# Attention and a gated MLP on one core: a list schedule with tuned ranks, and a literal order of all 2531 operations

## The chip, the core and the metric

One core of a Trainium2 chip runs the whole kernel as one program. Its engines run side by side, each in the order of its own instructions: TensorE (PE in the profile) multiplies matrices into PSUM, VectorE (DVE) and ScalarE (ACT) work element by element, GpSimd (POOL) does some elementwise work from SBUF, and SyncE (SP) issues the DMAs. They wait for one another by semaphores. The metric is the device time of one execution in microseconds.

## The reference

Inputs: q, k, v of (4, 8, 576, 64): four batches, eight heads, 576 positions, 64 channels; weights w_gate and w_val (512 x 1536) and w_out (1536 x 512), all fp32.

- q and k are rotated by position (RoPE: halves x1, x2 become x1 cos - x2 sin, x1 sin + x2 cos);
- scores = q k^T / 8, softmax over keys, times v, for each of the 32 heads;
- the heads are joined to x of 2304 x 512;
- out = (sigmoid(x w_gate) * (x w_val)) w_out, 2304 x 512.

## The kernel before, in words

**Numbers.** Nearly all matrix products run in fp16 with a high and a low half of each operand (three products a term), and each half is made by two elementwise steps: a "high" step that scales and rounds (line 476 on ACT or line 478 on DVE) and a "rest" step that subtracts (line 482, always DVE). Batch 0 is special: its scores and its first GLU half run on fp32 operands, while the weights are still being decoded.

**Stages.** For each batch b and head pair p, `keys_queries` loads q and k with a swapped copy, multiplies by cos (line 703, for batch 0 line 695) and by sin (705; batch 0 makes the swapped copy by a matrix product, line 690, and line 692), adds (707; 697), finds a scale (714, 717), splits into halves and moves them into `stk` by DMA. `attention` takes row tiles t of 128 queries: scores (765), a row minimum on DVE (788), exp on ACT (793), the sum's reciprocal on DVE (797, 799), high and rest of the probabilities (`softmax`, the call at 803), a transposing DMA into `pt` (944), then 30 products with v into the one PSUM bank `pv` (953) and its eviction on ACT and DVE. `hidden(b, f, i)` makes one of 12 blocks of the GLU for half i of a batch's tokens: 12 products for the gate into a bank of `m` (three banks), tanh on ACT (1018), 12 products for the value into another bank, (1 + tanh) * value on DVE (1021), high (the call at 1027) and rest. `project` makes one 128-token tile of the output, 36 products (1046), eviction, DMA out. For batch 0 the first half of the queries goes through `front` and `back` (lines 822 to 928): row maxima (826), a bias product (842, 876), transposed scores (881), exp (887), products with v and with ones (902), a reciprocal (912) and x in fp32 (914, 928). Meanwhile `w_in_chunk` loads 12 chunks of 1 MB of the two input weights, which arrive as 64-bit words, decodes them in two ACT-or-DVE passes (488; 496 on ACT or 493 on DVE) and a DVE join (500), and squares them on PE (519) for a scale (`w_in_scales`); `w_out_decode` does the same for w_out.

**What sets the order.** Nothing is issued as the functions run. Every operation is registered in a `Plan` with its engine, a rank, the tokens that it reads and writes, and a function that issues it; there are 2531. `Plan.order` is a list schedule: it steps through time with costs written in the kernel (`c_dve`, `c_act` and so on), and each engine that is free takes the ready operation of lowest rank. The ranks are those of the calls, moved by a table `SHIFT` of 285 numbers, one for each call of a stage function; `LEAD` moves loads; `SIDE` has a bit for each operation that may run on either of two engines (`alt`: ACT or DVE for a high step, GpSimd or DVE for the rotations). `emit` then issues the operations in the order of their planned starts. The buffers of five pools (`m`, `s`, `p32`, `th`, `p16`) are handed out as the plan goes. On the chip the planned times have no force: each engine has its list, and semaphores for the data.

Of the kernel before, what the change touches and what calls it, by code (L numbers as in the profile page):

```python
# [61 lines left out]
class Plan:  # L62


    HOP = 0.036
    TAIL = {"DVE": 0.085, "ACT": 0.1, "POOL": 0.05, "PE": 0.165, "SP": 0.0}
    OWN = {"DVE": 0.12, "POOL": 0.13}
    ENTER, LEAVE, SWAP = 0.096, 0.2, 0.25
    FIRST, WINDOW = 1.9, 3.41333

    def __init__(self):
        self.tasks, self.preds, self.wrote, self.read = [], [], {}, {}
        self.leases = []
        self.shift, self.side, self.alts, self.lead = 0.0, 0, 0, 0.0

    def add(self, where, rank, reads, writes, fn, land=0.0, port=False, also=(), mode=None):


        n = len(self.tasks)
        rank += self.shift  # L80
        held = {x for x in (*reads, *writes, *also) if isinstance(x, Lease)}
        for x in held:
            x.users.append(n)
        self.leases.append(held)
        pre = set()
        for r in reads:
            if r in self.wrote:
                pre.add(self.wrote[r])
        for w in (*writes, *also):
            if w in self.wrote:  # L90
                pre.add(self.wrote[w])
            pre.update(self.read.get(w, ()))
        for r in reads:
            self.read.setdefault(r, []).append(n)
        for w in writes:
            self.wrote[w], self.read[w] = n, []
        pre.discard(n)
        self.tasks.append((where, rank, fn, land, port, mode))
        self.preds.append(sorted(pre))

    def order(self):
        N = len(self.tasks)
        succ = [[] for _ in range(N)]
        left = [len(p) for p in self.preds]
        for n, p in enumerate(self.preds):
            for m in p:
                succ[m].append(n)
        free, wait, ready, done = {}, {}, {}, [None] * N
        slots, parked = {}, {}
        for held in self.leases:  # L110
            for x in held:
                slots.setdefault(x.pool, {n: 0.0 for n in range(len(x.bufs))})
                x.left = len(x.users)

        def obtain(n, t):

            need = {}
            for x in self.leases[n]:
                if x.n is None:
                    need.setdefault(x.pool, []).append(x)  # L120
            late = t
            for pool, xs in need.items():
                best = sorted((f, k) for k, f in slots[pool].items())[:len(xs)]
                if len(best) < len(xs):
                    parked.setdefault(pool, []).append(n)
                    return None
                late = max(late, best[-1][0])
            if late > t:
                return late
            for pool, xs in sorted(need.items()):  # L130
                for x, (f, k) in zip(sorted(xs, key=lambda x: x.users[0]), sorted((f, k) for k, f in slots[pool].items())):
                    x.n = k
                    del slots[pool][k]
            return t

        def release(n):
            for x in self.leases[n]:
                x.left -= 1
                if not x.left:
                    slots[x.pool][x.n] = max(done[m][1] + done[m][2] + self.TAIL[done[m][0]] for m in x.users) + self.HOP  # L140
                    for m in parked.pop(x.pool, []):
                        offer(m)

        def offer(n):
            for e, _ in self.tasks[n][0]:
                t = 0.0
                for m in self.preds[n]:
                    e0, end, land = done[m]
                    if land:
                        end += land + self.HOP  # L150
                    elif e0 == e:
                        end += self.OWN.get(e, 0.0)
                    else:
                        end += self.TAIL[e0] + self.HOP
                    t = max(t, end)
                heapq.heappush(wait.setdefault(e, []), (t, self.tasks[n][1], n))
                ready.setdefault(e, [])
                free.setdefault(e, 0.0)

        for n in range(N):  # L160
            if not left[n]:
                offer(n)
        starts, bus, drain, port, last = [], self.FIRST, 0.0, 0.0, None
        slow, busy = {0: True}, {}

        def run(t, cost):

            w = int(t / self.WINDOW)
            while cost > 1e-9:
                if w not in slow:  # L170
                    k = max(slow)
                    while k < w:
                        x = busy.get(k, 0.0) / self.WINDOW
                        slow[k + 1] = x < (0.46 if slow[k] else 0.25)
                        k += 1
                u = min(cost, max(0.0, (w + 1) * self.WINDOW - t) * (0.5 if slow[w] else 1.0))
                busy[w] = busy.get(w, 0.0) + u
                cost -= u
                t += u * (2.0 if slow[w] else 1.0)
                w += 1  # L180
            return t
        while len(starts) < N:
            best = None
            for e in free:
                w, r = wait[e], ready[e]
                while w and done[w[0][2]]:
                    heapq.heappop(w)
                while r and done[r[0][1]]:
                    heapq.heappop(r)
                if r or w:  # L190
                    t = free[e] if r else max(free[e], w[0][0])
                    if best is None or t < best[0]:
                        best = (t, e)
            t, e = best
            w, r = wait[e], ready[e]
            while w and w[0][0] <= t:
                _, rank, n = heapq.heappop(w)
                if not done[n]:
                    heapq.heappush(r, (rank, n))

            held = e in ("DVE", "POOL") and port > t + 0.2
            fit = [x for x in r if not held or (e == "DVE" and not self.tasks[x[1]][4])]
            if fit:
                x = min(fit)
                r.remove(x)
                heapq.heapify(r)
            else:
                x = heapq.heappop(r)
            n = x[1]
            got = obtain(n, t)  # L210
            if got != t:
                if got is not None:
                    heapq.heappush(w, (got, x[0], n))
                continue
            where, rank, fn, land, locks, mode = self.tasks[n]
            cost = dict(where)[e]
            if e == "PE":
                if mode != last:
                    t += self.ENTER if last is None else self.LEAVE if mode is None else self.SWAP
                last = mode  # L220
            if e == "POOL" or (e == "DVE" and locks):
                t = max(t, port)
                port = t + cost
            end = run(t, cost) if e == "PE" else t + cost
            if land:

                if mode:
                    bus = max(bus, t + 1.1, drain - 0.3) + land[0]
                    end = max(end, drain + 0.1)
                else:  # L230
                    bus = max(bus, t + 1.0) + land[0] * (0.67 if t < 40 else 1.0)
                    drain = max(drain, bus + land[1])
                done[n] = (e, end, bus + land[1] - end)
            else:
                done[n] = (e, end, 0.0)
            free[e] = end
            starts.append((t, n, e))
            release(n)
            for m in succ[n]:
                left[m] -= 1  # L240
                if not left[m]:
                    offer(m)
        self.done = done
        return sorted(starts)

    def emit(self):
        self.starts = self.order()
        for t, n, e in self.starts:
            self.tasks[n][2](e)


# [79 lines left out]
def rope_attention_then_sigmoid_glu(ctx: ExitStack, tc: tile.TileContext, qk, v, w_in, w_out, tables, out):  # L331
# [59 lines left out]
    P = Plan()  # L391
# [14 lines left out]
    def op(e, us, rank, reads, writes, fn, port=False):  # L406
        P.add(((e, us),), rank, reads, writes, lambda _: fn(eng.get(e)), port=port)
# [14 lines left out]
    def dma(rank, reads, writes, kb, fn, also=(), load=False, more=0.0):  # L422
        if load:
            rank += P.lead
# [239 lines left out]
    slots = {}  # L664
# [560 lines left out]
```

## Time and profile before

| | us |
|---|---|
| median of 3 runs (664.24 to 665.35) | 665.19 |
| the profiled execution | 665.45 |
| its span, first to last instruction | 663.7 |
| PE busy in the span | 638.0 |
| DVE busy | 515.1 |
| ACT busy | 345.5 |
| POOL busy | 79.8 |

An engine's busy time is the union of its instructions. The rows further down name an engine, a line of the kernel, what is written from what is read, and a count; a bracket behind a row gives the engine's idle time ahead of it and who ended it.

### The profile page before, as it was taken

What the parts mean: (1) busy time and instruction counts of PE and PEld (TensorE: products, weight loads), DVE (VectorE), ACT (ScalarE), POOL (GpSimd) and SP (SyncE); (2) the same over time, 40 slices, a digit from 0 to 9 for tenths busy, and PEclk for the clock granted to TensorE, in tenths of its full rate; (3) what the DMA queues carried; (4) which work ended last, traced back from release to release, by engine and by line L of the source; (5) the groups of instructions that cost most, each with busy time, mean ns of one, the idle gap of its engine ahead of it and who ended that gap; (6) DMA issues with size and microseconds to landing.
All of it is one profiled execution on the core that took longest, in us unless ns stands there. A gap on an engine that the chain in (4) does not pass through costs nothing.

```text
span 663.7 us, 12849 instructions
## 1 busy us (share of the span) xinstructions
PE 638.0 (96%) x4914; PEld 439.8 (66%) x4914; DVE 515.1 (78%) x1211; ACT 345.5 (52%) x711; POOL 79.8 (12%) x85
## 2 busy tenths in 40 slices
PE   5799989999999999999999999999999999999998
PEld 2455567777776558876776557876765578877645
DVE  3999799989999989989899579868868788533100
ACT  1787548747576577645245556426525566311200
POOL 4132000110213200114200010134000000000000
PEclk9989999999999999999999999999999999999999
DMA  8986447852598676997347896862454585300010
GB/s 322 411 306 249 128 138 199 188 127 48 150 168 230 161 161 154 195 186 170 104 85 173 183 176 153 181 156 67 100 126 88 120 179 99 90 1 1 1 48 32
DMA packets 172524, 97.10 MB, mean 146 GB/s; under 512 B 152880, under 2 KB 161584, under 8 KB 170544
## 3 DMA queue, kind: packets, MB, share of 16 engines
q1 hardware_dynamic: 172464, 96.29, 58.3%
q8 instruction: 38, 0.62, 0.4%
q14 instruction: 22, 0.18, 0.1%
HBM read 40.83 MB, written 4.72 MB: 69 GB/s over the span
## 4 chain that ended last, share of the span: by engine, by line
PE 55%; DMA 5%; DVE 2%; ACT 0%; issue 0%; DVEq 0%; SPq 0%; ACTq 0%
PE m L1004 31%; PE m L1046 13%; PE pv L953 6%; PE s L765 5%; DMA pt<-p 3%; DMA xt<-in_v_dram 1%; DVE p L482 1%; DMA p<-p 1%; DVE p L788 1%; DVE p L478 0%; PE m L465 0%; ACT sink L714 0%; ACT p L793 0%; DVE th L1021 0%; DVE v L478 0%
## 5 line engine op out<-in xcount | busy, mean ns | idle before, releaser
L1004 PE MATMUL m<-xt,w 128*128 128x320 f16 (+1 forms) x2016 | 258.8, 288 | 0.0
L1004 PEld LDWEIGHTS <-w 128*128 128x128 f16 x2016 | 196.1, 98 | 55.8 <-issue 2.6
L1046 PE MATMUL m<-wo,gt 128*128 128x512 f16 (+1 forms) x684 | 145.5, 368 | 0.0
L793 ACT ACTIVATE p<-p,st 128x576 f32<-128x576 f32 x128 | 98.6, 771 | 69.8 <-DVE p L788 65.7
L1046 PEld LDWEIGHTS <-gt 128*128 128x128 f16 x684 | 66.5, 98 | 67.8 <-issue 1.1
L482 DVE SCALAR_TENSOR_TENSOR p<-p,st,p 128x576 f16<-128x576 f32 x128 | 100.1, 812 | 4.8 <-ACT p L476 4.2
L788 DVE TENSOR_SCALAR_CACHE_REDUCE p<-s,q_e 128x576 f32<-128x576 f32 x108 | 85.7, 809 | 7.3 <-PE s L765 6.6
L1018 ACT ACTIVATE th<-m,gsc 128x320 f32<-128x320 f32 (+1 forms) x84 | 41.9, 499 | 75.3 <-PE m L1004 75.1
L1021 DVE SCALAR_TENSOR_TENSOR th<-th,m 128x256 f32<-128x256 f32 (+1 forms) x96 | 42.8, 448 | 38.7 <-PE m L1004 38.0
L765 PE MATMUL s<-stk 128*128 128x288 f16 (+1 forms) x480 | 65.9, 287 | 0.3 <-DVE p L788 0.3
L476 ACT ACTIVATE p<-p,st 128x576 f16<-128x576 f32 x67 | 50.4, 767 | 20.4 <-DMA pt<-p 8.1
L953 PE MATMUL pv<-pt,v 128*64 128x320 f16 (+1 forms) x840 | 57.6, 289 | 1.7 <-DMA pt<-p 1.6
L953 PEld LDWEIGHTS <-v 128*64 128x64 f16 x840 | 46.2, 110 | 13.0 <-issue 7.7
L765 PEld LDWEIGHTS <-stk 128*128 128x128 f16 (+1 forms) x480 | 42.5, 101 | 17.0 <-issue 4.0
L482 DVE SCALAR_TENSOR_TENSOR gt<-th,gt 128x320 f16<-128x320 f32 (+1 forms) x84 | 41.7, 498 | 6.6 <-ACT gt L476 5.9
L1000 PE MATMUL m<-xt,w 128*128 128x256 f32 x176 | 41.6, 386 | 0.3 <-DVE w_m L527 0.3
L478 DVE TENSOR_SCALAR p<-p,st 128x576 f16<-128x576 f32 x61 | 33.5, 557 | 5.8 <-DMA pt<-p 5.2
L1000 PEld LDWEIGHTS m<-xt,w 128*128 128x128 f32 x176 | 32.3, 190 | 7.4 <-issue 1.1
L703 POOL TENSOR_TENSOR qk<-qk,tab 128x576 f32<-128x576 f32 x11 | 17.8, 1633 | 158.9 <-DMA qk<-in_qk_dram 84.0
L705 POOL TENSOR_TENSOR sw<-sw,tab 128x576 f32<-128x576 f32 x13 | 21.1, 1631 | 109.9 <-ACT o L476 50.2
L476 ACT ACTIVATE xt<-pv 128x320 f16<-128x320 f32 (+1 forms) x28 | 11.5, 411 | 36.0 <-PE pv L953 33.0
L476 ACT ACTIVATE gt<-th 128x320 f16<-128x320 f32 (+1 forms) x36 | 16.0, 444 | 24.9 <-DVE th L1021 24.9
(159 smaller groups left out, 661.4 us busy)
## 6 DMA issues: line engine op xcount, KB each, us to landing
wo<-in_w_dram SPq DMA_DIRECT2D x12, 1024.0 KB, 8.6
qk<-in_qk_dram SPq DMA_DIRECT2D x12, 576.0 KB, 6.0
sw<-in_qk_dram SPq DMA_DIRECT2D x12, 576.0 KB, 5.0
xt<-in_wo_dram SPq DMA_DIRECT2D x12, 512.0 KB, 3.7
stk<-sw SPq DMA_DIRECT2D x24, 216.0 KB, 3.6
stk<-sw SPq DMA_DIRECT2D x72, 72.0 KB, 2.7
out_dram<-o SPq DMA_DIRECT2D x15, 256.0 KB, 2.0
xt<-in_v_dram SPq DMA_DIRECT2D x3, 1152.0 KB, 5.2
```

The costliest lines, as they stand in the source:

```text
L476: A.activation(o, src, AF.Copy, scale=scale)
L478: E.tensor_scalar(out=o, in0=src, scalar1=scale, scalar2=1.0, op0=ALU.mult, op1=ALU.mult)
L482: V.scalar_tensor_tensor(out=o, in0=src, scalar=scale, in1=hi, op0=ALU.mult, op1=ALU.subtract)
L765: T.matmul(o[:, c, 0:288], lhsT=q[:, rows:rows + width], rhs=kk[:, c * 288:c * 288 + 288], start=(m == 0), stop=(m == 1))
L788: lambda E, h=h, c=c: V.tensor_scalar(out=prs[c]().rearrange("p (c n) -> p c n", c=2), in0=h()[:, :, 0:288], scalar1=down, scalar2=None, o ...
L793: lambda E, c=c: A.activation(prs[c](), prs[c](), AF.Exp, bias=st[:, k, 0, c:c + 1], scale=-1.0, accum_out=st[:, k, 1, c:c + 1]))
L953: T.matmul(v_ps[64 * e:64 * e + 64, 0:n], lhsT=v16[:, p, a, j + 5 * e, :], rhs=pt[z][:, c * 9 + g, 0:n], start=(first and m == 0), stop=(l ...
L1000: T.matmul(halves(m()[:, 0:n]), lhsT=raw[g][:, 128 * cc:128 * cc + 128], rhs=x32[cc], start=(cc == 0), stop=(cc == NP - 1))
L1004: T.matmul(m()[:, 0:n], lhsT=w16[:, f, g, a, cc, :], rhs=x[:, cc, c, c0:c0 + n], start=(k == 0), stop=(k == 11))
L1018: op("ACT", c_act(n), rank - 0.05, [m] + S0, [r], lambda E, m=m: A.activation(t(), m()[:, 0:n], AF.Tanh, scale=gate))
L1021: op("DVE", c_dve(n, psum=True), rank - 0.05, [m], [r], lambda E, m=m: V.scalar_tensor_tensor(out=t(), in0=t(), scalar=1.0, in1=m()[:, 0:n ...
L1046: T.matmul(m()[:, 0:w], lhsT=gt[:, f, a, c0:c0 + 128], rhs=wo16[:, f, x, c:c + w], start=(f == 0 and k == 0), stop=(f == NF - 1 and k == 2))
```

## The change

The planner, its costs, the ranks and the tables `SHIFT` and `LEAD` go. `Plan.add` keeps the engine and the function; `emit` walks a literal list `ORDER` of the 2531 operations. `CALLS` gives the order in which the 285 stage calls register their operations (which numbers them, and so sets the dependencies), and `SIDE` is a new table of the engine bits. Pool buffers are handed out, at an operation's place in the list, to the first buffer released.

```
     def emit(self):
+        slots, left = {}, {}
+        for held in self.leases:
+            for x in held:
+                slots.setdefault(x.pool, [(n - len(x.bufs), n) for n in range(len(x.bufs))])
+                left[x] = len(x.users)
+        for k, n in enumerate(ORDER):
+            where, fn = self.tasks[n]
+            for x in sorted((x for x in self.leases[n] if x.n is None), key=lambda x: x.users[0]):
+                x.n = heapq.heappop(slots[x.pool])[1]
+            fn(where)
             for x in self.leases[n]:
+                left[x] -= 1
+                if not left[x]:
+                    heapq.heappush(slots[x.pool], (k, x.n))
...
+CALLS = (
+    0, 1, 2, 16, 8, 6, 9, 17, 7, 68, 70, 21, 69, 20, 3, 29, 4, 42, 19, 22, 11, 31, 73, 10, 270, 30, 14, 34, 65, 44, 25,
...
+ORDER = (
+    0, 4, 6, 13, 2, 30, 49, 35, 42, 261, 9, 53, 78, 3, 7, 64, 10, 16, 8, 11, 14, 31, 12, 18, 15, 17, 20, 36, 22, 21, 23,
...
-    calls = [(c[0] + k / 1000.0, n, k / 1000.0) for n, (c, k) in enumerate(zip(todo, SHIFT))]
-    for _, n, P.shift in sorted(calls):
-        P.side, P.alts, P.lead = SIDE[n], 0, LEAD[n] / 1000.0
+    for n in CALLS:
+        P.side, P.alts = SIDE[n], 0
         todo[n][1](*todo[n][2])
```

The computation, the tiles and the instructions are the same, but for the engine of those that have a choice. Counted from the tables (the stage functions are unchanged, so each number of `ORDER` can be traced to its operation), the two lists compare like this:

| operations | before | after |
|---|---|---|
| on PE / SP | 584 / 267 | 584 / 267 |
| on DVE / ACT / POOL | 1083 / 542 / 55 | 1060 / 574 / 46 |
| rotations on POOL (lines 695 to 707) | 38 | 29 |
| softmax high step on DVE, of 128 | 61 | 52 |
| GLU high step on DVE, of 96 | 53 | 36 |
| GLU pairs with another user of an `m` bank between gate and value | 2 of 96 | 48 of 96 |
| GLU pairs with the value's products first | 0 | 14 |
| changes of PE's tiling (full, row or column halves) along PE's list | 119 | 110 |
| of these behind the first product of batch 0's second GLU half | 50 | 48 |

A PE operation stands on average 2 places from where it was, at most 21; an ACT operation 17 places, a DVE operation 15. The queue of SP begins before with qk of pair 0, two 64 KB pieces (`turned`, `ident`), the tables, qk of pairs 1, 3, 2, weight chunks 3, 5, v of pairs 0, 2, chunk 4; after with `turned`, qk of pairs 0, 1, the tables, chunk 3, v of pair 0, chunks 5, 4, a 512 KB block of w_out, v of pair 2, qk of pair 3, `ident`, qk of pair 2. On ACT the first operations before are a tanh of one column and a copy of `ident`; after they stand fifth and ninth, behind passes over chunks 3, 5 and 4. In the ACT list after, the second pass over chunk 3 stands behind the first pass over chunk 5.

## Rows read from the trace of the kernel before

**Rows 1.** The page: busy us, share and instructions of an engine; the chain's shares.

```profile
PE 638.0 (96%) x4914; PEld 439.8 (66%) x4914; DVE 515.1 (78%) x1211; ACT 345.5 (52%) x711; POOL 79.8 (12%) x85
...
PE 55%; DMA 5%; DVE 2%; ACT 0%; issue 0%; DVEq 0%; SPq 0%; ACTq 0%
```

**Rows 2.** Windows by stage: length, then busy us (instructions) of PE, PEld, DVE, ACT, POOL.

```profile
0.00:25.73 25.73, 14.94 (x68) 8.39 (x68) 13.87 (x20) 9.54 (x12) 8.04 (x17) 1.00 0.93 353
25.73:71.00 45.27, 40.87 (x354) 24.95 (x356) 44.53 (x92) 35.35 (x58) 11.44 (x12) 0.96 0.78 286
71.00:88.91 17.91, 15.35 (x139) 9.14 (x135) 12.77 (x28) 7.43 (x16) 0.00 (x0) 1.00 0.37 111
88.91:160.00 71.09, 69.49 (x445) 51.85 (x445) 67.59 (x172) 50.91 (x112) 6.46 (x4) 1.00 0.61 153
160.00:621.30 461.30, 458.23 (x3701) 324.43 (x3700) 375.48 (x904) 238.15 (x509) 53.90 (x52) 1.00 0.60 132
```

**Rows 3.** Timeline of PE: start, length, line, and in brackets the idle time before.

```profile
149.91 1.99 PE L1000 MATMUL m<-xt,o 128*128 128x256 f32 x8 [1.25 <-DVE th L1021]
...
449.71 0.39 PE L465 MATMUL m<-q_m,ones 128*128 128x3 f32 x2 [1.09 <-ACT sink L714]
```

**Rows 4.** Timeline of DVE in the first 27 us, from its first row.

```profile
8.97 1.42 DVE L692 TENSOR_TENSOR sw<-s,tab 128x576 f32<-128x576 f32 x2 [8.97 <-PE s L690]
11.65 0.76 DVE L692 TENSOR_TENSOR sw<-s,tab 128x576 f32<-128x576 f32 x1 [1.26 <-PE s L690]
...
24.51 1.23 DVE L500 SCALAR_TENSOR_TENSOR w<-wo 128x1024 int32<-128x1024 int32 x1 [1.25 <-ACT wo L496]
...
25.73 0.75 DVE L692 TENSOR_TENSOR sw<-s,tab 128x576 f32<-128x576 f32 x1
```

**Rows 5.** DMA: the tables' issue (KB, us to landing); a window's last column is GB/s.

```profile
tab<-in_const_dram SPq DMA_DIRECT2D x1, 576.0 KB, 6.7
...
10.00:15.00 5.00, 3.45 (x16) 2.04 (x16) 3.55 (x5) 0.00 (x0) 4.00 (x2) 1.00 1.02 431
```

**Rows 6.** Timeline of ACT, its first row, and chunk 4's second pass.

```profile
0.74 1.28 ACT L1079 ACT_TABLE_LOAD   x1 [0.74 <-PEq L1215]
...
23.36 1.12 ACT L496 ACTIVATE wo<-wo 128x1024 uint32<-128x1024 uint32 x1
```

**Rows 7.** Groups by line: count, busy us, mean ns of one, idle before.

```profile
L703 DVE TENSOR_TENSOR qk<-qk,tab 128x576 f32<-128x576 f32 x13 | 9.6, 746 | 2.5 <-DMA qk<-in_qk_dram 2.5
L705 DVE TENSOR_TENSOR sw<-sw,tab 128x576 f32<-128x576 f32 x11 | 9.3, 848 | 1.1 <-issue 0.8 <-DMA sw<-in_qk_dram 0.3
...
L478 DVE TENSOR_SCALAR v<-xt,v_s 128x576 f16<-128x576 f32 x7 | 3.9, 574 | 0.0
...
L695 DVE TENSOR_TENSOR stk<-stk,tab 128x1152 f32<-128x1152 f32 x2 | 2.7, 1348 | 0.0
...
L493 DVE TENSOR_SCALAR xt<-xt 128x512 int32<-128x512 int32 x6 | 2.5, 422 | 0.0
L493 DVE TENSOR_SCALAR wo<-wo 128x1024 int32<-128x1024 int32 x3 | 2.1, 688 | 0.0
```

**Rows 8.** GpSimd beside DVE: two timeline rows, and GpSimd's late row.

```profile
127.38 3.23 POOL L703 TENSOR_TENSOR qk<-qk,tab 128x576 f32<-128x576 f32 x2 [70.65 <-DMA qk<-in_qk_dram]
...
129.27 1.36 DVE L797 TENSOR_SCALAR st<-st 128x3 f32<-128x3 f32 x1
...
444.86 3.18 POOL L707 TENSOR_TENSOR qk<-qk,sw 128x576 f32<-128x576 f32 x1 [10.02 <-DVE row L454]
```

**Rows 9.** PE full and column-tiled: the chain's row, then the timeline's starts.

```profile
274.87 6.55 PE m L1004 x60
...
274.71 6.71 PE L1004 MATMUL m<-xt,w 128*128 128x256 f16 x60
281.35 2.23 PE L953 MATMUL pv<-pt,v 128*64 128x320 f16 x30
```

**Rows 10.** Groups by line: the reader of a gate's bank.

```profile
L1018 ACT ACTIVATE th<-m,gsc 128x320 f32<-128x320 f32 (+1 forms) x84 | 41.9, 499 | 75.3 <-PE m L1004 75.1
```

More of the change, by code (lines that the diff above doesn't have):

```diff
@@ L62 @@
 class Plan:
[L65 to L69, printed above, removed]
-    def __init__(self):
[L72 to L81, printed above, removed]
+    def __init__(self):
+        self.tasks, self.leases, self.side, self.alts = [], [], 0, 0
@@ L82, in add @@
+    def add(self, where, tokens, fn):
+        held = {x for x in tokens if isinstance(x, Lease)}
         for x in held:
-            x.users.append(n)
+            x.users.append(len(self.tasks))
         self.leases.append(held)
[L85 to L109, printed above, removed]
+        self.tasks.append((where, fn))
@@ L110, in order, with emit @@
+    def emit(self):
+        slots, left = {}, {}
         for held in self.leases:
             for x in held:
[L112 to L117, printed above, removed]
-            for x in self.leases[n]:
[L119 to L249, printed above, removed]
-SHIFT = (
[21 rows of a table removed]
+                slots.setdefault(x.pool, [(n - len(x.bufs), n) for n in range(len(x.bufs))])
[5 more added lines that the diff above has]
+            fn(where)
+            for x in self.leases[n]:
+                left[x] -= 1
+                if not left[x]:
+                    heapq.heappush(slots[x.pool], (k, x.n))
@@ L274 @@
+CALLS = (
[12 rows of a table added]
 )
 SIDE = (
[15 rows of a table removed]
-)
-LEAD = (
[10 rows of a table removed]
[8 rows of a table added]
+)
+ORDER = (
[124 rows of a table added]
 )
@@ L406, in op @@
     def op(e, us, rank, reads, writes, fn, port=False):
-        P.add(((e, us),), rank, reads, writes, lambda _: fn(eng.get(e)), port=port)
+        P.add(e, (*reads, *writes), lambda _: fn(eng.get(e)))
     def op2(us, rank, reads, writes, fn):
@@ L422, in dma @@
     def dma(rank, reads, writes, kb, fn, also=(), load=False, more=0.0):
-        if load:
-            rank += P.lead
-        P.add((("SP", 0.62),), rank, reads, writes, lambda _: fn(), land=(kb / 250 + 0.15 + more if also else 0.2 + kb / 290 + more, 0.5), also=also)
+        P.add("SP", (*reads, *writes, *also), lambda _: fn())
     def transpose(rank, reads, writes, us, fn):
-        P.add((("SP", 1.9),), rank, reads, writes, lambda _: fn(), land=(us, 0.5), mode="T")
+        P.add("SP", (*reads, *writes), lambda _: fn())
     def mm(us, rank, reads, writes, fn, mode=None):
-        P.add((("PE", us),), rank, reads, writes, lambda _: fn(), mode=mode)
+        P.add("PE", (*reads, *writes), lambda _: fn())
     def tiny(rank, reads, writes, fn, us=0.085, port=False):
```

188 rows, old and new, of tables (CALLS, LEAD, ORDER, SHIFT) are left out of this document.

## The prediction

> **What bounds the kernel now.** I read the page's busy shares first, then the chain of waits, then a table of windows, then the timelines of the stretches where PE stands idle. The reader is to see there that PE is busy for 638.0 of 663.7 us and that the chain that ends last is PE for 55% of the span, more than all else in it [rows 1]. PE's work does not change, so the change can only move what PE waits. The windows say where that is [rows 2]: up to the first GLU product at 88.91 PE is idle for 25.73 - 14.94 = 10.8, 45.27 - 40.87 = 4.4 and 17.91 - 15.35 = 2.6 us; from there to 160 for 1.6 us; and in the 461 us behind that for 3.1 us. In the second window DVE is busy for 44.53 of 45.27 us: early on DVE is the engine that PE waits for. Later the waits are few: 1.25 us for DVE at 149.91 and 1.09 us for ACT at 449.71 are the two largest [rows 3].
>
> So the most that a new order can win is what PE idles behind its start, and the most that it can lose has no such bound: one engine's list is enough to make PE wait.
>
> **The start, to 25.73 us.** In SP's new queue 512 KB more lie ahead of the tables (pair 1's 576 KB come forward, 64 KB go back). At the 431 GB/s of the window from 10 to 15 us that is 0.52 MB / 431 = 1.2 us [rows 5]. DVE's first operation needs the tables; its start goes from 8.97 [rows 4] to 10.2. It then does two L692 (1.35 together, 0.67 from one start to the next) and an L695 that GpSimd did (1.35, [rows 7]), and the L697 of the same shape (1.27 to the next start) ends at 14.1. Up to the first L692 of pair 2 there follow two L692, seven L826 of the same length (9 x 0.67), one L697 (1.27), three joins L500 (1.23 less an overlap of 0.1, [rows 4]) and three small ones (0.23): 10.9 us, with some 0.2 for PSUM 25.2. Before it was 25.73, with gaps of 1.26 and 1.25 us in it [rows 4]. The second of these goes if chunk 4 is decoded in time: its 1 MB lie 1504 KB nearer the front of the queue (3.6 us at 431 GB/s), and ACT, which ended its second pass on it at 24.48 [rows 6], would end at 20.9, or 21.5 with the passes over chunk 5 that stand ahead of it; DVE comes to it at 23.1. DVE is then 0.5 us ahead, with one L695 more behind it. Bounds: if the tables are no later than before, 1.7 ahead; if they are late and chunk 4 keeps its gap, 0.7 late.
>
> One thing could spoil that margin. The tanh of one column stands first on ACT and has a table load of 1.28 us before it, the only one in the trace [rows 6]. In the new list four passes of other functions come first. If these are served by another table, the tanh needs a load of its own, just ahead of chunk 4: 1.28 us, decoded at 22.8, still before 23.1. I take nothing for it. The Trainium skill (ScalarE: Activation LUTs, What ACT_TABLE_LOAD costs) gives such a switch 2.66 us with its drain: chunk 4 would be ready at 24.2, DVE 1.1 us late, and the sum below 1.1 us worse. The trace has the load's own 1.28 us and no second load; whether a switch in mid-stream costs more, no run here shows yet.
>
> **From 25.73 to the first GLU product at 88.91.** That product needs the last x of pair 3 (L914 on DVE). What DVE has to do before it: two decode passes over 1 MB chunks (688 ns), three over 512 KB blocks (422), one L703 (746), one L697 (as L695, 1348) and two high steps (574) go to other engines; two passes (422), two high steps (574), the L695 and one L705 (848) come to it [rows 7]. Out 1.38 + 1.27 + 0.75 + 1.35 + 1.15 = 5.9, in 0.84 + 1.15 + 1.35 + 0.85 = 4.2: 1.7 us less, and 3.05 less without the L695 already counted. What ACT gets (seven operations for four) lies in time that it has: it is busy for 42.8 of these 63.2 us [rows 2]. If DVE set the end all the way, the product would come 3.05 us earlier here. But from 71 to 89 DVE is idle for 5.1 of 17.9 us [rows 2]; there a chain through loads, ACT, PE and the reciprocal decides, and PE's groups stand in almost the same order in both lists. I take half, 1.5. Bounds: 0 and 3.05.
>
> **From there to 160.** The 1.6 us of PE's idle time end on DVE for the most part [rows 2, 3]. GpSimd gives up 9 of its 38 rotations. How that matters is seen at 129.27: a three-column L797 takes 1.36 us while GpSimd's two L703 run [rows 8]. In PE's list the groups around the wait at 149.91 are dealt out anew. I take half: 0.8; bounds 0 and 1.6.
>
> **From 160 on.** The wait at 449.71 comes from a GpSimd L707 that took 3.18 us [rows 8], and ACT's L714 behind it. In the new list both L707 of that pair (batch 3, pair 1) are on DVE, and PE's waiting operation stands behind two score groups more: the 1.09 us go. The other 2.0 us I leave. The new list must add some waits of its own; I take 0.6. Together -0.5. Bounds: -3.1 (all idle time of the window) and +5.2 (the rival of the banks, below).
>
> **Smaller things.** PE's tiling changes 50 times behind the first product of batch 0's second GLU half, 48 times in the new list. Going into column tiles costs 281.35 - 274.71 - 6.55 = 0.09 us [rows 9]; for going out I take the same: -0.2. At the end the last tile's second half is finished behind tile 2 instead of alone; its eviction and DMA follow as before, with a 256 KB store just ahead instead of a 128 KB one long done: +0.1, between nothing and the 0.5 us of one more ACT operation [rows 10].
>
> **Sum.** -0.5 - 1.5 - 0.8 - 0.5 - 0.2 + 0.1 = -3.4 us. The profiled execution took 665.45, its span 663.7 with 1.75 around it; that gives 662.05. The median of the runs, 665.19, lies 0.26 below that execution, so I say 661.8.
>
> **Rivals.**
> (1) The idle time goes for good: DVE's relief comes through whole, and the two long stretches lose their waits. -0.5 - 3.05 - 1.6 - 3.1 - 0.2 = -8.4: 656.8. For it: early DVE is busy for 98% of the second window. Against it: that asks for no new wait among 584 PE operations.
> (2) Nothing that counts moves. PE's operations stand 2 places from their old ones on average, the chain from 71 to 89 is one of latencies, and new waits cancel the rest: -0.5 or so, 664.7. For it: only 3.1 us of idle time in the last 461 us. Against it: DVE's list before the first GLU product is shorter by sum.
> (3) Slower, by the three banks of `m`. Before, gate and value of a block stand next to each other in 94 of 96 cases; in the new list other users of the banks lie between them in 48, and in 14 the value's sum comes first and keeps its bank until the gate's tanh is done. Two banks are left for PE to alternate, and a group of 12 products of 256 columns takes 1.31 us (6.55 / 5, [rows 9]). The reader of the other bank, L1018 with 0.5 us [rows 10], must then start within some 0.8 us of the group's end; behind one ACT or DVE operation of that length PE waits. This decides from the point where readers stand later than that. If a quarter of the 46 new cases costs the reader's 0.5 us, that is 5.7 us: -3.4 + 5.7 = +2.3, 667.5. For it: DVE is busy for 81% and ACT for 52% of the time from 160 to 621, so a reader often finds its engine taken. Against it: before, PE waited for a bank's reader hardly ever there.
>
> **How the numbers follow.** A measurement of this kernel tells a change from none at about 0.2%, 1.33 us: faster is below 663.86, slower above 666.52. My forecast has 0.45 (659.3 to 663.8 is its own range), the first rival 0.15, the second 0.19, the third 0.21. Faster is the forecast and the first rival, 0.60; same 0.19; slower 0.21. The range runs from the first rival to just past the third, 656.3 to 667.8, and leaves out larger gains and worse stalls.
>
> **What would show it.** DVE's first row at about 10.2 and its fourth or later L692 of pair 2 near 25.2, without a gap before chunk 4's join; the first GLU product at about 86.9; from there to PE's last product 2 to 3 us less idle time; no PE wait of 1 us behind L714; about 29 rotations on GpSimd and fewer DVE operations stretched beside them. I am wrong if DVE's start delay lasts to 89 us, if a second table load costs chunk 4 its place, or if the windows from 160 on show more than 3.1 us of idle PE, with waits that end on L1018 or L1021. A time below 657 would mean that the latency chain before 89 us was DVE's after all.

## The result: faster by 0.9%, twice the gain forecast

The changed kernel takes 658.42 us (median of 5 runs, 657.62 to 660.41), the kernel before in the same comparison 665.19 (5 runs); the ratio is 0.991, with a 95% interval from 0.9886 to 0.9935. That is 6.8 us less, where the prediction had 3.4: 661.8, with a range from 656.3 to 667.8. The time lies in the range and outside the 659.3 to 663.8 of the likeliest case, nearer to the first rival's 656.8.

The page of the changed kernel, its line of busy times and the chain's shares, beside [rows 1]:

```profile
PE 637.0 (97%) x4914; PEld 440.8 (67%) x4914; DVE 508.7 (78%) x1188; ACT 357.0 (54%) x743; POOL 59.8 (9%) x76
...
PE 59%; DVE 2%; DMA 1%; issue 1%; ACT 1%; SPq 0%; ACTq 0%; DVEq 0%
```

PE has the same 4914 products in 7.5 us less span (656.2). DVE and GpSimd have less to do, ACT more, and DMA's share of the chain falls from 5% to 1%.

Line numbers are 60 lower than before (L1004 is L944, L953 is L893, L692 is L632). The windows, cut at the same operations as [rows 2]:

```profile
0.00:24.70 24.70, 15.38 (x72) 9.07 (x72) 15.04 (x19) 8.76 (x12) 5.58 (x16) 0.93 0.91 351
24.70:68.90 44.20, 40.07 (x347) 24.07 (x348) 41.21 (x87) 36.84 (x60) 12.13 (x11) 1.00 0.82 301
68.90:84.78 15.88, 15.23 (x141) 9.19 (x137) 13.97 (x29) 9.09 (x18) 0.00 (x0) 1.00 0.40 121
84.78:155.42 70.64, 69.99 (x451) 52.98 (x450) 65.49 (x175) 53.58 (x116) 5.14 (x5) 1.00 0.66 155
155.42:613.80 458.38, 457.22 (x3697) 324.44 (x3696) 371.29 (x879) 244.59 (x533) 36.91 (x44) 1.00 0.57 133
```

Length and PE's busy time stand first in each line; their difference is PE's idle time. Stage by stage:

| stage (before) | length before, after | gain | PE idle before, after |
|---|---|---|---|
| to 25.73 | 25.73, 24.70 | 1.03 | 10.79, 9.32 |
| to 71.00 | 45.27, 44.20 | 1.07 | 4.40, 4.13 |
| to the first GLU product, 88.91 | 17.91, 15.88 | 2.03 | 2.56, 0.65 |
| to 160 | 71.09, 70.64 | 0.45 | 1.60, 0.65 |
| to 621.3 | 461.30, 458.38 | 2.92 | 3.07, 1.16 |

The gains add up to 7.5 us. The stages hold slightly different operations (the lists differ), so idle time is the safer column behind 88.91: 4.67 us before, 1.81 after.

Each profile is of one execution, and executions of the same lists differ. Of the kernels below, e2 has the lists of the kernel before up to the first GLU product, and e1, e5 and e7 have those of the changed kernel. Windows up to that product, first e2, then e1:

```profile
0.00:87.51 87.51, 69.55 (x556) 41.40 (x556) 70.77 (x136) 52.61 (x85) 21.84 (x29) 1.00 0.74 274
```

```profile
0.00:85.28 85.28, 71.02 (x556) 42.40 (x556) 70.97 (x135) 54.88 (x88) 18.15 (x29) 0.98 0.76 282
```

So the old lists reach the product at 88.91 and 87.51, the new ones at 84.78, 85.28, 85.38 (e5) and 84.55 (e7). The gain there is between 2.1 and 4.4 us, and none of the three stage gains ahead of 88.91 is good to better than about 1 us.

Where PE waited, beside [rows 3]; the first fence is of the kernel before, a row not shown yet, the second of the changed one:

```profile
88.25 0.38 PE L457 MATMUL m<-row,ones 1*128 1x6 f32 x2 [1.35 <-DVE row L454]
```

```profile
84.46 0.38 PE L397 MATMUL m<-row,ones 1*128 1x6 f32 x2 [0.40 <-DVE row L394]
...
183.04 0.43 PE L944 MATMUL m<-xt,w 128*128 128x320 f16 x2 [0.69 <-DVE th L961]
...
445.70 0.28 PE L405 MATMUL m<-q_m,ones 128*128 128x3 f32 x2
```

The wait just ahead of the first GLU product shrinks by 0.95 us, the one at 449.71 (445.70 now) is gone, and the largest that is left behind the first product has 0.69 us.

### The profile page after: what moved, and what is told of

Its sections match the earlier page's. It is cut to its first block, busy times and chain, and to the rows that moved or that the text cites. A ratio compares the mean times of both kernels' runs of the same rounds, so it can differ in the third digit from the quotient of the medians.

```text
span 656.2 us, 12825 instructions
## 1 busy us (share of the span) xinstructions
PE 637.0 (97%) x4914; PEld 440.8 (67%) x4914; DVE 508.7 (78%) x1188; ACT 357.0 (54%) x743; POOL 59.8 (9%) x76
## 4 chain that ended last, share of the span: by engine, by line
PE 59%; DVE 2%; DMA 1%; issue 1%; ACT 1%; SPq 0%; ACTq 0%; DVEq 0%
PE m L944 31%; PE m L986 16%; PE s L705 6%; PE pv L893 6%; DMA pt<-p 1%; DMA stk<-sw 1%; DVE p L422 0%; DVE p L728 0%; DVE p L418 0%; DVE gt L422 0%; ACT p L416 0%; ACT p L733 0%; ACT o L416 0%; DVE th L961 0%; DVE sw L422 0%
## 5 line engine op out<-in xcount | busy, mean ns | idle before, releaser
L944 PE MATMUL m<-xt,w 128*128 128x320 f16 (+1 forms) x2016 | 259.7, 288 | 0.8 <-DVE th L961 0.7
L944 PEld LDWEIGHTS <-w 128*128 128x128 f16 x2016 | 196.3, 98 | 56.4 <-issue 3.2
L422 DVE SCALAR_TENSOR_TENSOR p<-p,st,p 128x576 f16<-128x576 f32 x128 | 105.4, 841 | 8.1 <-ACT p L416 7.1
L961 DVE SCALAR_TENSOR_TENSOR th<-th,m 128x256 f32<-128x256 f32 (+1 forms) x96 | 43.1, 450 | 39.8 <-PE m L944 29.7
L416 ACT ACTIVATE p<-p,st 128x576 f16<-128x576 f32 x76 | 57.3, 768 | 26.8 <-DVE st L739 10.1
L705 PE MATMUL s<-stk 128*128 128x288 f16 (+1 forms) x480 | 68.9, 287 | 0.4 <-DMA stk<-sw 0.2
L893 PE MATMUL pv<-pt,v 128*64 128x320 f16 (+1 forms) x840 | 58.5, 289 | 0.0
L893 PEld LDWEIGHTS <-v 128*64 128x64 f16 x840 | 46.1, 110 | 10.8 <-issue 7.1
L416 ACT ACTIVATE gt<-th 128x320 f16<-128x320 f32 (+1 forms) x52 | 22.4, 437 | 30.0 <-DVE th L961 30.0
L416 ACT ACTIVATE o<-m,o_s 128x512 f32<-128x512 f32 (+1 forms) x17 | 11.1, 651 | 37.9 <-PE m L986 34.8
L643 POOL TENSOR_TENSOR qk<-qk,tab 128x576 f32<-128x576 f32 x10 | 15.1, 1522 | 173.9 <-DMA qk<-in_qk_dram 76.7
L418 DVE TENSOR_SCALAR p<-p,st 128x576 f16<-128x576 f32 x52 | 29.8, 578 | 1.2 <-DMA pt<-p 0.4
L733 ACT ACTIVATION_READ_ACCUMULATOR p<-p,st 128x1 f32 x128 | 24.0, 188 | 0.0
```

What stands on the lines that cost most here:

```text
L416: A.activation(o, src, AF.Copy, scale=scale)
L418: E.tensor_scalar(out=o, in0=src, scalar1=scale, scalar2=1.0, op0=ALU.mult, op1=ALU.mult)
L422: V.scalar_tensor_tensor(out=o, in0=src, scalar=scale, in1=hi, op0=ALU.mult, op1=ALU.subtract)
L705: T.matmul(o[:, c, 0:288], lhsT=q[:, rows:rows + width], rhs=kk[:, c * 288:c * 288 + 288], start=(m == 0), stop=(m == 1))
L733: lambda E, c=c: A.activation(prs[c](), prs[c](), AF.Exp, bias=st[:, k, 0, c:c + 1], scale=-1.0, accum_out=st[:, k, 1, c:c + 1]))
L893: T.matmul(v_ps[64 * e:64 * e + 64, 0:n], lhsT=v16[:, p, a, j + 5 * e, :], rhs=pt[z][:, c * 9 + g, 0:n], start=(first and m == 0), stop=(l ...
```

## The experiments

The twelve kernels ran in three sets on three chips, on which the kernel before has a median of 666.4 to 667.1 us and spreads from 662 to 675.5. So each is judged by its ratio to the kernel before in the same set (6 to 12 executions of each new kernel, 23 to 29 of the kernel before), with intervals of 0.003 to 0.004 to either side (the prediction counted on 0.2%), and by its profile. The profile is of one execution, and that can be slow for its kernel (e9's is the slowest of nine). In the lists below, "front" is all that stands ahead of the first GLU product: 342 operations in the new order, 345 in the old.

| kernel | ratio, 95% interval | first GLU product at | PE idle from there to the last projections |
|---|---|---|---|
| before | 1 | 88.91 | 4.67 |
| changed | 0.991, 0.9886 to 0.9935 | 84.78 | 1.81 |
| e1 new front, old rest | 0.9957, 0.993 to 0.9985 | 85.28 | 6.04 |
| e2 old front, new rest | 0.9941, 0.991 to 0.9972 | 87.51 | 3.12 |
| e3 new loads alone in front | 1.0196, 1.0152 to 1.024 | 101.35 | 7.20 |
| e4 new engines' lists alone in front | 0.9989, 0.9957 to 1.0021 | 90.21 | 5.90 |
| e5 e1 and five waits moved | 0.9957, 0.9925 to 0.9989 | 85.38 | 5.15 |
| e6 29 rotations back | 0.9955, 0.9922 to 0.9988 | 89.20 | 3.22 |
| e7 pairs joined | 1.041, 1.0369 to 1.0452 | 84.55 | 33.21 |
| e8 tables first | 0.989, 0.985 to 0.993 | 88.38 | 2.26 |
| e9 one rotation back | 0.9906, 0.9872 to 0.9939 | 90.26 | 2.22 |
| e10 one rotation new | 0.9983, 0.995 to 1.0016 | 87.03 | 8.93 |
| e11 new order, old engines | 1.0094, 1.0063 to 1.0125 | 86.75 | 8.70 |
| e12 old order, new engines | 1.015, 1.011 to 1.0191 | 91.17 | 9.90 |

**Do the two halves add? (e1, e2)**

```diff
 ORDER = (
-    (0 to 344 old) (the rest old)
+    (0 to 341 new, with new engines) (the rest old, old engines)      # e1
+    (0 to 344 old, old engines) (the rest new, with new engines)      # e2
```

> The first 342 operations of the new list (all that stands ahead of the first GLU product), with their engines, and behind them the old list with the old engines. Theory (the gain is made stage by stage and adds up): the first GLU product comes at 84.8 as in the changed kernel, all behind it runs as before, and the whole takes 665.2 - 4.1 = 661.1 us. Rival (the early gain is given back: what stalls behind the first product is set by loads, transposes and GpSimd, which do not come earlier): 664 us or more, with more idle time of PE behind 84.8 than the kernel before has behind 88.9.

> The other half: the old list up to the first GLU product (345 operations), the new one behind it. Theory: the first GLU product at 88.9, and 658.4 + 4.1 = 662.5 us, so a gain of 2.7 us on the kernel before that comes from the removed waits behind the first product alone. Rival (the later part gains only because the early part leaves it time): 664.5 us or more.

e1 gains 0.43%, e2 0.59%; 0.9957 x 0.9941 = 0.990, the changed kernel's 0.991 within the intervals. Both halves gain by themselves, as the theory has it. In us of 665.19 that is 2.9 for the front, where 4.1 was expected, and 3.9 for the rest, where 2.7 was. The 4.1 was itself read off one execution of each kernel; against e2, e1's first product comes only 2.2 us earlier. The table shows a second place where e1 can lose, as its rival has it: PE idles 6.04 us behind the first product, 1.4 more than before. e2 has 1.3 more there than the changed kernel, with the same list; whether a half loses by its new partner or executions scatter by so much, two profiles don't tell. Windows from the first GLU product on, first e1, then e2:

```profile
85.28:615.00 529.72, 523.68 (x4108) 372.92 (x4109) 441.99 (x1070) 287.30 (x616) 59.95 (x56) 1.00 0.60 135
```

```profile
87.51:615.00 527.49, 524.37 (x4119) 374.81 (x4120) 435.01 (x1049) 297.66 (x647) 41.80 (x47) 1.00 0.58 136
```

**What in the front makes its gain? (e3, e4)**

```diff
 SP's list
-pair 0, turned, ident, tables, pairs 1, 3, 2, chunks 3, 5, values 0, 2, chunk 4, w_out 0, ...
+turned, pairs 0, 1, tables, chunk 3, values 0, chunks 5, 4, w_out 5, values 2, pair 3, ident, pair 2, ..., w_out 0
```

e3 makes this edit alone; e4 leaves SP's list old and takes the other four engines' new lists.

> The kernel before with the new order of the loads alone (the 20 places of SP's list that differ ahead of the first GLU product); PE, DVE, ACT and GpSimd keep their old lists. Theory (DVE's list sets the front, loads little): chunk 4 comes earlier and the 1.25 us gap of DVE ahead of 25.73 goes, but little else: first product at 87.9, time 664.2 us. Rival (the loads set the front): first product at 85 to 86, 661 to 662 us. If the tables come later by what stands ahead of them, 0.5 to 1 us worse than before: 665.7 to 666.2.

> The counterpart: the old order of the loads, the new order and the new engines of PE, DVE, ACT and GpSimd ahead of the first GLU product, the old list behind it. Theory: most of the front's gain is here, 3 us: first product at 85.9, time 662.2 us. Rival (the loads set the front): the engines wait for loads that come in the old order, first product at 88 or later, 664.5 to 666 us.

None of the expectations held for e3: it is 13 us slower. Its timeline, of GpSimd, DVE, PE and ACT in order of time (idle time before a row in brackets):

```profile
9.28 5.19 POOL L635 TENSOR_TENSOR stk<-stk,tab 128x1152 f32<-128x1152 f32 x2 [6.78 <-PE s L630]
...
11.94 3.75 DVE L637 TENSOR_TENSOR stk<-stk,sw 128x1152 f32<-128x1152 f32 x1 [0.46 <-POOL stk L635]
...
15.74 0.85 PE L762 MATMUL s<-stk 64*128 64x288 f32 x2 [4.08 <-DVE stk L637]
...
40.69 0.65 ACT L428 ACTIVATE xt<-xt 128x512 f32<-128x512 f32 x1 [12.67 <-DMA xt<-in_wo_dram]
...
41.66 0.40 PE L816 MATMUL s<-o,onesb 64*128 64x256 bf16 x2 [6.19 <-ACT o L789]
```

Two old choices meet the new loads. Pair 1 now lands early, so GpSimd does two L635 on end, and DVE's L637 stands beside the second: 3.75 us, where it takes 1.35 alone. And ACT's old list comes to a block of w_out that the new queue has moved back; ACT waits 12.67 us with everything behind it. In e4 it is the other way round. ACT, DVE and PE of e4:

```profile
18.15 1.14 ACT L428 ACTIVATE wo<-wo 128x1024 f32<-128x1024 f32 x1 [1.56 <-DMA wo<-in_w_dram]
...
20.31 1.22 DVE L440 SCALAR_TENSOR_TENSOR w<-wo 128x1024 int32<-128x1024 int32 x1 [2.42 <-ACT wo L436]
...
21.59 0.50 PE L459 MATMUL m<-w 128*128 128x128 bf16 x3 [2.60 <-DVE w L440]
```

ACT's new list puts the first pass over chunk 5 ahead of the second over chunk 3; the old queue lands chunk 5 late, and chunk 3, which is there, waits behind it, with DVE's join and PE. So the front's gain is in neither part; it is in their fit. The theory that the engines' lists carry 3 us of it fell, if narrowly (e4's interval begins at 0.9957, where 0.9955 was expected), and so did the one that the loads do.

**Are the removed waits the gain behind the first product? (e5)**

```diff
 PE's list, behind e1's front
-hidden f6, hidden f11 gate, score, [149.91] hidden f11 value, ..., score
+hidden f6, hidden f11 gate, score, score, hidden f11 value, ...
-[342.19] weigh, [375.77] weigh, [449.71] sum of q, [513.47] weigh
+the same four, each behind the one or two groups that followed it
```

> The kernel of e1 (new front, old list behind it) with five edits of PE's list alone, at the five largest waits that the kernel before has behind its first GLU product: a score group moved ahead of the second product of the pair that waits at 149.91, and the waiting groups at 342.19, 375.77, 449.71 and 513.47 each put one or two groups later. Theory (the gain behind the first product is these few waits, and PE has other work to put there): 0.65 + 0.33 + 0.64 + 1.09 + 0.66 = 3.4 us less than e1, a ratio of 0.9957 - 0.0051 = 0.991 to the kernel before, as the changed kernel has. Rival (the engines behind the waits are late as a whole, so the waits come back a group later): within 0.001 of e1's 0.9957.

The rival held: 0.9957, as e1. The waits for transposes that e1 has near 339, 374 and 511 go or shrink to 0.16, that at 146 from 1.25 to 0.75. But others grow or are new. Timeline of PE in e5:

```profile
153.14 0.46 PE L893 MATMUL pv<-pt,v 128*64 128x320 f16 x4 [0.63 <-DMA pt<-p]
...
204.23 0.46 PE L893 MATMUL pv<-pt,v 128*64 128x320 f16 x4 [0.55 <-DMA pt<-p]
...
398.03 0.63 PE L893 MATMUL pv<-pt,v 128*64 128x256 f16 x8 [0.92 <-DMA pt<-p]
```

One of the five waits is not in e1 at all: there is none of the sum of q, but one of 1.09 us for L961 at 434.60, of which e5 keeps 0.85. Idle time falls from 6.04 to 5.15 us, where 3.4 less were hoped for, and the changed kernel has 1.81 there; by the ratio nothing is won. A wait that is read off a row is not worth its length: what feeds PE is late at several places, and the group put in its stead comes to the next one early.

**Which of the two, order or engines? (e11, e12)**

```diff
-order old, engines old
+order new, engines old      # e11
+order old, engines new      # e12
```

> The new order of all operations with every one of the 175 that changed engine on its old engine. Theory (order and engines are found together, and either alone breaks what the other counts on): no gain or a loss, ratio 0.998 to 1.02. Rival (the order is the gain): 0.991 to 0.994.

> The old order with the 175 operations on their new engines (DVE 6.4 us less, GpSimd 20 less, ACT 11.5 more). Theory: as for the order alone, ratio 0.998 to 1.02. Rival (DVE's relief is the gain, wherever it stands): 0.992 to 0.995.

Both lose, 0.94% and 1.5%, as the theory has it, and together they gain 0.9%. Their windows from the first GLU product on, e11 and e12:

```profile
86.76:620.00 533.24, 524.54 (x4113) 373.81 (x4113) 445.98 (x1070) 283.28 (x616) 57.37 (x58) 1.00 0.57 135
```

```profile
91.17:630.00 538.83, 528.93 (x4113) 374.17 (x4114) 436.14 (x1051) 301.34 (x647) 42.90 (x47) 1.00 0.59 133
```

PE's idle time is 8.70 and 9.90 us, about twice that of the kernel before. e12 has DVE's relief (436.14 us busy behind the first product, against 445.98 in e11), and it helps nothing without the order.

**Rotations on GpSimd (e6, e9, e10)**

```diff
-all 29 rotations that changed engine: new      # changed kernel
+all 29 on their old engines                    # e6
+SIDE[2] = 1: L635 of batch 0's pair 0 on GpSimd, the other 28 new      # e9
+the kernel before, with that one on DVE        # e10
```

> The changed kernel with the 29 rotation operations (L635, L637, L643, L645, L647) that changed engine put back on their old engine, 19 to GpSimd and 10 to DVE, at their places in the new list; all else as changed. Theory (GpSimd's relief is part of the gain: its rotations hold DVE up and some, as in batch 3's pair 1, come late): the 3 us rotations beside DVE come back, 1.5 to 3 us slower than the changed kernel, ratio 0.993 to 0.995. Rival (the order of the lists alone makes the gain): 0.990 to 0.991 as the changed kernel.

> The changed kernel with one operation of 2531 put back on its old engine: the rotation L635 of batch 0's pair 0, on GpSimd instead of DVE. Theory (this one is what makes the new order of the loads usable: with pair 1 loaded early, GpSimd's next rotation follows at once and DVE's L637 stands beside it): a wait of 5 us at PE near 16, the first GLU product 3.5 to 4.1 us later, ratio to the kernel before 0.996 to 0.998. Rival (what e6 lost it lost by the other 28 operations): 0.991 to 0.992 as the changed kernel.

> The counterpart: the kernel before with that one rotation of pair 0 (L695 there) on DVE, loads and all other lists old. Theory (the operation is worth something only with the new order of the loads): pair 1 is loaded late, so GpSimd's next rotation does not fall beside DVE's L697 anyway; 0 to 0.7 us less, ratio 0.999 to 1.000. Rival (this operation alone is the front's gain): 3 to 4 us less, 0.994 to 0.996.

e6 loses about half the gain: 0.9955, just past what the theory gave it, with an interval that still overlaps the changed kernel's. Its profile shows the loss in the front, 89.20 against 84.78, and 1.4 us more idle time behind. In e9 the profile does what the theory said; POOL, DVE and PE:

```profile
9.68 5.21 POOL L635 TENSOR_TENSOR stk<-stk,tab 128x1152 f32<-128x1152 f32 x2 [7.18 <-PE s L630]
...
12.34 3.76 DVE L637 TENSOR_TENSOR stk<-stk,sw 128x1152 f32<-128x1152 f32 x1 [1.95 <-POOL stk L635]
...
16.82 0.85 PE L762 MATMUL s<-stk 64*128 64x288 f32 x2 [5.14 <-DVE sw L632]
```

But its ratio is 0.9906, as the changed kernel, and the interval shuts out the 0.996 that this wait should cost. The profiled execution is the slowest of nine (663.86, median 661.59, two at 657.7), so what the others did in these 17 us isn't known: that one rotation decides the front is not shown. e10 came as its theory has it, 0.9983 with an interval around 1; its profiled execution has a wait of 3.44 us for a transpose at 208.32 (e3 has one of 2.78 at 223.82, e4 one of 1.12 at 209.54, the kernel before none there), and I read nothing else from it.

**The banks of m (e7)**

```diff
 PE's list of the changed kernel, 48 places
-hidden gate f, (another user of m), hidden value f
+hidden gate f, hidden value f, (another user of m)
```

> The changed kernel with 48 of its 50 separated gate and value pairs put next to each other again on PE (the second of a pair moved up to the first, where the lists allow it, else the first down to the second); the other engines' lists as changed. Theory (a bank held longer costs nothing, the new list has its readers in time): no gain, the same to 1 us slower, ratio 0.990 to 0.993. Rival (the separation costs readers' time at the banks, and the gain would be larger without it): 1 to 2 us faster than the changed kernel, 0.987 to 0.989.

Neither held: 4.1% slower, with 33.2 us of idle PE behind the first product. PE's timeline in e7 near the end:

```profile
642.45 1.79 PE L944 MATMUL m<-xt,w 128*128 128x320 f16 x12 [0.62 <-ACT th L958]
...
644.89 1.79 PE L944 MATMUL m<-xt,w 128*128 128x320 f16 x12 [0.65 <-DVE th L961]
```

PE waits in turn for the tanh and for the product that read the sums before, some 0.6 us each time, as if it had one bank. The likely reason, not tested by itself: the readers stand in the new lists' order, and they free the banks in that order. So banks can cost what the third rival feared, and more; but it is the joined pairs that pay, against lists made for separated ones.

**Earlier tables (e8)**

```diff
 SP's list of the changed kernel
-turned, pair 0, pair 1, tables, chunk 3, ...
+tables, turned, pair 0, pair 1, chunk 3, ...
```

> The changed kernel with the load of the tables first in SP's list, ahead of the small load and of pairs 0 and 1 (it was fourth). In four kernels so far the tables landed 6.5 to 6.7 us behind their issue at 2.13, whatever stood ahead. Theory (the landing follows the issue): issued at 0.75 they land at 7.3 to 7.5, DVE starts 1.2 us earlier, and as DVE works without a gap until 21 us the first GLU product comes 0.8 to 1.2 us earlier: ratio 0.988 to 0.989. Rival (the bytes decide: pairs 0 and 1 come later by the 576 KB put ahead): PE's first products 0.5 us or more later, DVE waits for them instead, same or 0.5 us slower, 0.990 to 0.992.

PE and DVE in e8, their first rows:

```profile
8.38 1.30 PE L630 MATMUL s<-stk,o 128*128 128x288 f32 x2 [8.38 <-DMA stk<-in_qk_dram]
```

```profile
10.68 0.76 DVE L632 TENSOR_TENSOR sw<-s,tab 128x576 f32<-128x576 f32 x1 [10.68 <-PE s L630]
```

The theory fell: pair 0, issued at 1.65 instead of 1.19, lets PE start at 8.38 instead of 5.52, 2.9 us later, and DVE waits for PE. The first GLU product comes 3.6 us later in this execution. The ratio, 0.989 on six executions, is what the theory forecast and can't be told from the changed kernel's; if it is a gain, not by the theory's way. None of the twelve is shown to beat it.

## Why the prediction had the sign and half the size

**The start, -0.5: it was -1.03.** The sum held that the tables (cos and sin) come 1.2 us later, so that DVE starts at 10.2. That step failed. DVE's first row in the changed kernel, then the row ahead of chunk 4's join, the join and the row that ends the stage, beside [rows 4]:

```profile
8.70 1.62 DVE L632 TENSOR_TENSOR sw<-s,tab 128x576 f32<-128x576 f32 x2 [8.70 <-DMA tab<-in_const_dram]
...
22.16 0.76 DVE L766 TENSOR_REDUCE m<-s 128x2 f32<-128x576 f32 x1 [0.57 <-PE s L762]
22.84 1.22 DVE L440 SCALAR_TENSOR_TENSOR w<-wo 128x1024 int32<-128x1024 int32 x1
...
24.70 0.75 DVE L632 TENSOR_TENSOR sw<-s,tab 128x576 f32<-128x576 f32 x1
```

The tables were not late at all: 8.70 against 8.97, issued at 2.13 us in both. What was right: chunk 4's gap of 1.25 us is gone. With the tables in time the prediction's bound was 1.7 ahead. The 0.57 us for which DVE waits at 22.16 is most of what is missing: there PE runs at the lower clock (0.53 from 19.70 to 23.10, see the last section). In e5, with the same lists and a granted clock of 1.00, that wait is absent and the stage ends 1.64 us ahead:

```profile
24.09 0.75 DVE L632 TENSOR_TENSOR sw<-s,tab 128x576 f32<-128x576 f32 x1
```

So the -0.5 was off by the 1.2 us for the tables, and the lower clock hid half of the miss.

**From 25.73 to the first product, -1.5: it was -3.10 in the profiled executions.** The bound was 3.05, but DVE's relief did not come through whole. By the windows, DVE's busy time in these two stages fell by 2.12 us (57.30 to 55.18), not by 3.05, and its idle time by 0.98 (5.88 to 4.90). The half was taken off because "a chain through loads, ACT, PE and the reciprocal decides" from 71 to 89. Just there the stage gained most, 2.03 us, and its idle time of PE fell from 2.56 to 0.65. How much of the 3.10 belongs to the change is open: from the row that ends the first stage to the first GLU product, the old lists take 63.18 us (before) and 61.99 (e2), the new ones 60.08 (changed), 60.77 (e1), 61.29 (e5) and 59.92 (e7). The gain is 0.7 to 3.3 us, and 1.5 lies in that. That the relief did it is only argued: e12 has the relief and no gain, so it takes the new order too.

**To 160, -0.8: idle time fell by 0.95.** Right: the wait at 149.91 is gone. Which of the two causes named did it, GpSimd's relief or the new order of PE's groups there, was not separated.

**From 160 on, -0.5: it was -2.92, of which 1.91 is idle time.** This is the term that was most mis-sized, and the ratio bears it out: e2, with the new list behind the first product alone, gains 3.9 us (1.9 to 6.0 by its interval), where the prediction's terms for that part add up to 1.4. The step that failed is "the other 2.0 us I leave". All of the old waits went, not only that at 449.71; the new ones, taken as 0.6, are 1.16 together, the largest at 183.04 [0.69]. GpSimd and DVE ahead of it:

```profile
178.62 1.40 POOL L645 TENSOR_TENSOR sw<-sw,tab 128x576 f32<-128x576 f32 x1 [5.27 <-DMA sw<-in_qk_dram]
180.10 1.40 POOL L647 TENSOR_TENSOR qk<-qk,sw 128x576 f32<-128x576 f32 x1
```

```profile
179.09 1.12 DVE L418 TENSOR_SCALAR gt<-th 128x320 f16<-128x320 f32 x1
180.24 1.61 DVE L422 SCALAR_TENSOR_TENSOR gt<-th,gt 128x320 f16<-128x320 f32 x1
```

DVE's two operations take 1.12 and 1.61 us beside the rotations, against 0.36 and 0.53 on average for this shape, and the L961 that PE waits for stands behind them. This is the mechanism of [rows 8], now with fewer such rotations (29, as predicted).

**Smaller things.** PE's busy time up to the last product fell by 1.0 us (637.97 to 636.98); the tiling's 0.2 is in it and can't be told apart. The tail behind the last product is the same, 3.3 us, for the +0.1.

**The tanh's table.** ACT's rows, beside [rows 6]:

```profile
0.74 1.28 ACT L428 ACT_TABLE_LOAD   x1 [0.74 <-PEq L1154]
...
17.57 0.19 ACT L1019 ACTIVATE sink<-zero 128x1 int8<-128x1 f32 x1
```

One load serves all; it now stands ahead of the first decode pass, and the tanh at 17.57 needs none. The Trainium skill's price of a switch (ScalarE: Activation LUTs, What ACT_TABLE_LOAD costs) was not put to the test, since there was no switch.

**The rivals.** The first, all idle time for good, came nearest: 7.5 of its 8.4 us came in the profiled executions, 6.8 by the medians. That it "asks for no new wait among 584 PE operations" was the argument against it, and PE does wait for 1.81 us behind the first product. The second, new waits cancel the rest, is what e5 does; the whole change doesn't. The third, the banks, shows in the changed kernel in waits of 0.69 and 0.11 us at L944, not 5.7. So the sign was right, and PE's waits fell in every stage, as said. The size was cut twice: by half of DVE's relief, for which the prediction had a row (DVE idle for 5.1 of 17.9 us), and by 2.0 of the 3.1 us from 160 on, for which it had none. The second cut was a guess that waits would come back, and a list made as a whole did not bring them back. That the first was wrong is not shown.

## What to carry to other kernels

An order of operations, the engines that they run on and the order of the loads are one thing: here each alone brought nothing or lost up to 2%, and together they gain 0.9%. Don't price such a change as a sum of its moves, nor test it by undoing one, without asking which other list counts on that move; and don't leave idle time out of the sum without a row that says why it must stay. Before explaining a stage's gain, read it off a second execution of the same lists: here the same front differed by 1.4 us. Moving a waiting operation a little back is worth much less than its wait (0.9 us of idle time for 3.4 in e5, and nothing by the ratio).

## What the runs showed of the hardware

**A load's landing is not the bytes ahead of it.** The tables, issued at 2.13 us, land 6.7, 6.6 and 5.7 us later in the old queue (before, e4, e10) and 6.5, 6.4 and 6.0 later in the new one (changed, e3, e9), with 512 KB more ahead. But issued first they land after 3.8 us, and pair 0 came 2.9 us later with these 576 KB ahead of it (e8). What decides is left open.

**One DVE operation beside GpSimd can cost 2.4 us:** L637 took 1.35 us alone and 3.75 or 3.76 beside an L635 on GpSimd that had started 0.08 or 0.07 us before it and took its usual 2.61 (e3, e9). In the changed kernel DVE's L637 starts first, at 11.62, and takes 1.36; there GpSimd's L635, from 11.80, takes 3.67 us. In these pairs the one that starts second pays.

**The granted clock behind a wait.** In e9 PE stood still for 5.14 us until 16.82, and then had the lower level, 1.2 GHz, up to 26.3. Windows of e9 (the fourth value from the end is POOL's, then the granted clock):

```profile
10.00:16.80 6.80, 1.68 (x7) 0.78 (x5) 4.85 (x4) 3.84 (x4) 4.88 (x2) 0.96 1.02 417
16.80:26.30 9.50, 8.58 (x36) 4.79 (x36) 7.84 (x10) 3.56 (x7) 0.00 (x0) 0.50 0.65 236
```

The changed kernel has 0.53 from 19.70 to 23.10, behind waits of 1.98 and 1.17 us, and the kernel before 0.57 and 0.58 from 36 to 40, where the longest wait in the 8 us ahead is 0.75. But e5, with the front of the changed kernel, has the same waits and the full clock; PE's rows and a window:

```profile
13.74 1.42 PE L762 MATMUL s<-stk 64*128 64x288 f32 x8 [2.03 <-DVE sw L632]
...
17.36 1.42 PE L762 MATMUL s<-stk 64*128 64x288 f32 x8 [1.17 <-DVE stk L637]
```

```profile
4.00:64.00 60.00, 50.33 (x382) 30.08 (x382) 52.37 (x91) 41.27 (x64) 16.09 (x13) 1.00 0.91 344
```

The clock goes with the scatter: e9's two executions at a mean clock of 1.000 took 657.7 us, its five at 0.992 took 661.0 to 663.9. So a wait in the front costs its own length and sometimes the clock behind it; for waits of 1 to 2 us nothing here shows when. The prediction had no term for that, though the 0.96 in the second row of [rows 2] shows it.
